# Two buffers for the exponents of weight halves, and their sums in the PSUM buffer of the weighted values, in an attention and feed-forward kernel

## The chip, the cores and the metric

The kernel runs on one core of one Trainium2 chip. The metric is the device time of one execution in microseconds (us). The change is judged by the median of several runs against the kernel before.

## What is computed

The reference draws `q`, `k`, `v` of 8 batches, 8 heads, 576 rows and 64 columns in fp32, and three weights `w_gate` and `w_val` (512 x 1536) and `w_out` (1536 x 512), and computes

```python
scores = (1 / 8) * q @ k.T                          # per batch and head
kth    = 32nd largest of each row of scores
attn   = softmax over the entries >= kth
x      = (attn @ v), heads side by side             # 4608 x 512
out    = (sigmoid(x @ w_gate) * (x @ w_val)) @ w_out
```

The weights reach the kernel as float64, two 32-bit words for each number.

## The kernel before, in words

The engines are TensorE (PE; its weight loads are the separate row PEld), VectorE (DVE), ScalarE (ACT), GpSimd (POOL) and SyncE (SP), which issues most loads. Each has an instruction queue of its own and works through it in order.

**Attention.** A step is one tile of 128 query rows of two heads. PE forms the scores (`pss`, L298 or L316), ACT evicts them (`s`, L302 or L324), DVE finds the leading values (L394 to L400), ACT and POOL count and mask what lies under them (L407, L413, L414), DVE takes the 32nd largest (`kths`, L421), ACT and DVE form the masked exponentials (`e`, L332, L337), and PE transposes them (`pt`, L432), which ACT evicts into a ring (L438). When the tiles of a block are there, `weigh` multiplies them by the values on PE into the PSUM tile `po` (L480, L481). DVE reads `po` and divides by the row sums (`xf`, L485), and ACT and POOL split the result into a high part `xh` (L504) and a rest `xl` (L505).

**Feed-forward network.** For 384 tokens at a time PE forms `pz` (L540 to L542), ACT and DVE evict it (L547, L550), ACT and POOL split the product (L551, L552), and PE multiplies by the output weights (`po_0_0_0` and the like, L564 to L566).

**Splitting the weights.** There are 18 weight tiles of two halves each, 36 halves in all, and each is split once, in the first 245 us or so. One half is 128 x 512 numbers of two words, loaded by SP into `wraw` (three buffers). `split_front` works on it as follows: ACT scales the upper word (`wbits`, L190), DVE shifts it into place and puts in the sign (L191, L192), DVE cuts the exponent out of it into the tile `wpower` (L193), ACT turns the lower word into a number (L195), POOL multiplies that number by the exponent in two pieces (L197), and ACT takes the high part (L198). `split_back` sums on PE in three matmul groups into one PSUM tile `wrest`: the bits times the identity (L205), the high part times -1 (L206), and the product of POOL times 2^-52 (L207). ACT evicts the sum (L209, issued with high priority), and the finished half is stored to DRAM (L210).

**PSUM.** The pool `ps_f` has three buffers and holds, in turn, `wrest`, `pz` and the output product of the network. The pool `ps_o` has one buffer and holds the weighted values `po` of `weigh` (L464). A new tile waits until the reader of the buffer's last tile has finished: L209 for `wrest`, L547 or L550 for `pz`, L485 for `po`.

**Order of the work.** The order on PE is written by hand (`tc.manual_schedule`): `split_back` is called between other pieces of work, and its three groups stand in PE's order where it is called. The order on ACT, DVE, POOL and SP is found by a scheduler, which takes into account when buffers come free and which calls are marked `urgent()`.

Of the kernel before, what the change touches and what calls it, by code (L numbers as in the profile page):

```python
# [10 lines left out]
F32 = mybir.dt.float32  # L11
# [3 lines left out]
F32R = mybir.dt.float32r  # L15
BF16 = mybir.dt.bfloat16
FP8 = mybir.dt.float8e4
AF = mybir.ActivationFunctionType
# [12 lines left out]
def tile_topk_attention_then_gated_ffn(  # L31
# [8 lines left out]
    nc = tc.nc  # L40
    P = 128
    B, H, _, S = k.shape
# [10 lines left out]
    M = NP * P  # L53
# [36 lines left out]
    bi = ctx.enter_context(tc.tile_pool(name="bi", bufs=4))  # L90
    b2 = ctx.enter_context(tc.tile_pool(name="b2", bufs=2))
    bk = ctx.enter_context(tc.tile_pool(name="bk", bufs=2 * NP))
    bv = ctx.enter_context(tc.tile_pool(name="bv", bufs=3))
    bs = ctx.enter_context(tc.tile_pool(name="bs", bufs=4))
    bq = ctx.enter_context(tc.tile_pool(name="bq", bufs=3))
    bqr = ctx.enter_context(tc.tile_pool(name="bqr", bufs=4))
    bkr = ctx.enter_context(tc.tile_pool(name="bkr", bufs=2))
# [6 lines left out]
    ps_o = ctx.enter_context(tc.tile_pool(name="ps_o", bufs=1, space=bass.MemoryType.PSUM))  # L104
    ps_f = ctx.enter_context(tc.tile_pool(name="ps_f", bufs=3, space=bass.MemoryType.PSUM))

    ident = const.tile([P, P], F32, tag="ident", name="ident")
# [26 lines left out]
    def behind_scores():  # L134
        return tc.issue_after(evicted[-1].ins) if len(evicted) < 12 else ExitStack()

    def urgent():
        return tc.high_priority() if stated else ExitStack()
# [10 lines left out]
    stored, splits, waiting, fetched, ticks, evicted, due, later, pinned, raw_loads = set(), {}, [], {}, [0], [], [], [], [], []  # L149

    pre = ExitStack()
    pre_pools = {n: pre.enter_context(tc.tile_pool(name=n, bufs=bufs)) for n, bufs in (("signs", 1), ("raw", 3), ("parts", 3), ("power", 1))}
    plus, minus = [pre_pools["signs"].tile([P, P], F32R, tag=t, name=t) for t in ("plus", "minus")]
    nc.scalar.activation(plus, ident, AF.Copy, scale=2.0**-52)
    nc.scalar.activation(minus, ident, AF.Copy, scale=-1.0)

    split_order = order[KEPT:LOADED] + order[:KEPT] + order[LOADED:]
# [10 lines left out]
    def load_raw(idx, i):  # L168
        raws[idx, i] = raw = pre_pools["raw"].tile([P, NP * P, 2], U32, tag="raw", name=f"wraw_{idx}_{i}")
        ins = load(raw.rearrange("p n t -> p (n t)"), w[idx][:, i * NP * P : (i + 1) * NP * P].bitcast(U32))  # L170
        raw_loads.append(ins.ins)

    def split_front(idx, i):

        if i == 0:
            splits[idx] = pools["w"].tile([P, 2, 2, NP, P], F32R, tag="w", name=f"wsplit_{idx}")
        at = halves_of_weights.index((idx, i))
        for ahead in halves_of_weights[at : at + 2]:
            if ahead not in raws:
                load_raw(*ahead)  # L180
        raw = raws[idx, i]
        low, top = raw[:, :, 0], raw[:, :, 1]
        pair = splits[idx][:, i].rearrange("p a c n -> p a (c n)")
        bits = pre_pools["parts"].tile([P, NP * P], F32, tag="bits", name=f"wbits_{idx}_{i}")
        frac = pair[:, 1]
        word = bits.bitcast(U32)
        power = pre_pools["power"].tile([P, NP * P], BF16, tag="power", name=f"wpower_{idx}_{i}")
        heads = bits.bitcast(U16).rearrange("p (n t) -> p n t", t=2)[:, :, 1]
        with behind_scores():
            nc.scalar.activation(bits, top.bitcast(F32), AF.Copy, scale=2.0**-112)  # L190
        nc.vector.tensor_scalar(word, word, 3, None, op0=ALU.logical_shift_left)  # L191
        nc.vector.scalar_tensor_tensor(word, top, 0x80000000, word, op0=ALU.bitwise_and, op1=ALU.bitwise_or)  # L192
        nc.vector.tensor_scalar(power.bitcast(U16), heads, 0xFF80, None, op0=ALU.bitwise_and)  # L193
        with behind_scores():
            nc.scalar.activation(frac, low, AF.Copy)  # L195
        for c in (slice(0, 2 * P), slice(2 * P, 4 * P)):
            nc.gpsimd.tensor_tensor(frac[:, c], frac[:, c].bitcast(F32), power[:, c], op=ALU.mult)  # L197
        nc.scalar.activation(pair[:, 0], bits, AF.Copy)  # L198
        waiting.append((idx, i, pair, bits, ticks[0]))

    def split_back():
        idx, i, pair, bits, _ = waiting.pop(0)
        frac = pair[:, 1]
        rest = ps_f.tile([P, M], F32, tag="f", name=f"wrest_{idx}_{i}")
        nc.tensor.matmul(rest, ident, bits, start=True, stop=False)  # L205
        nc.tensor.matmul(rest, minus, pair[:, 0], start=False, stop=False)  # L206
        nc.tensor.matmul(rest, plus, frac, start=False, stop=True)  # L207
        with urgent():
            nc.scalar.activation(pair[:, 1], rest, AF.Copy)  # L209
        nc.scalar.dma_start(w_split[idx][:, i], pair.bitcast(F32))  # L210
        if i == 1:
            stored.add(idx)
# [23 lines left out]
    def next_front():  # L236
        while len(waiting) > 2:
            split_back()
        split_front(*due.pop(0))
# [94 lines left out]
    def masked(J, s, kth, st, e, nm, place=None):  # L334

        for j in range(J):
            nc.vector.scalar_tensor_tensor(  # L337
                e[:, j], s[:, j], kth[j], e[:, j], op0=ALU.is_ge, op1=ALU.mult, accum_out=st[:, 4 + j : 5 + j]
            )
        nc.vector.tensor_scalar(st[:, 4 : 4 + J], st[:, 4 : 4 + J], 1e-9, None, op0=ALU.add)  # L340
        if place is not None:
            x, k, rows = place
            invs = inverses[x]
            sums = st[:, 4:6] if J == 2 else st[:, 4:5].to_broadcast([P, 2])
            nc.vector.reciprocal(invs[:, k:8:4], sums)
            if k == 3:
                turned_invs = b6[0].tile([P, 32], F32, tag="invt", name=f"invt_{nm}")
                nc.vector.transpose(turned_invs, invs)
                for x in range(4):
                    nc.sync.dma_start(rows[:, 32 * x : 32 * x + 32], turned_invs[32 * x : 32 * x + 8])  # L350
            return e, None
        nc.vector.reciprocal(st[:, 6 : 6 + J], st[:, 4 : 4 + J])
        inv = bi.tile([P, P], F32, tag="inv", name=f"inv_{nm}")
        nc.gpsimd.tensor_copy(
            inv.rearrange("p (j d) -> p j d", j=J), st[:, 6 : 6 + J].unsqueeze(2).to_broadcast([P, J, P // J])
        )
        return e, inv
# [19 lines left out]
    def select(J, s, col, nm, place):  # L377
# [42 lines left out]
        for j in range(J):  # L420
            nc.vector.max(kths[:, at[j] : at[j] + 8], u[:, j])  # L421
        yield masked(J, s, [kths[:, a + 7 : a + 8] for a in at], st, e, nm, place)

    def turn(e, inv, i, et, nm):
# [85 lines left out]
    def ffn(nm0, xs, t0, width, early, last):  # L510
# [7 lines left out]
        def load(idx):  # L518
            if not (t0 == 0 and early):
                return stored_weight(idx, nm0)  # L520
            first_weights(order.index(idx))
            while idx not in stored:
                if not waiting:
                    next_front()
                split_back()
            return fetched[idx]
# [72 lines left out]
    def run(general):  # L599
# [160 lines left out]
        for n in range(len(steps) + 3):  # L760
# [6 lines left out]
            if splitting:  # L767
                split_front(*fronts.pop(0))
# [24 lines left out]
            else:  # L793
# [9 lines left out]
                for t, chunk in enumerate(chunks):  # L803
                    ticks[0] += 1
                    if not fronts and not splitting:
                        if waiting and ticks[0] - waiting[0][4] > 3:
                            split_back()
                        if due and len(waiting) < 3:
                            next_front()
                    if chunk is not None:  # L810
                        next(chunk, None)
                        while unfinished and t == 0:
                            weighted(*unfinished.pop(0))
                    elif 3 <= n:
                        weighed(n - 3)
                        if n == OPEN:
                            weighed(n - 2)
                    if t == 2 and splitting and len(waiting) > 1:
                        split_back()
                    if n != OPEN or t > 0:  # L820
                        more(begun + (goal - begun) * (t + 1) / len(chunks))
# [84 lines left out]
```

## Time and profile before

| quantity | value |
|---|---|
| median of 3 runs | 1576.34 us |
| lowest and highest run | 1575.83 and 1578.79 us |
| the profiled execution's own time | 1575.44 us |
| its span in the profile | 1573.6 us |
| PE busy, share of the span | 1500.9 us, 95% |
| DVE busy | 1289.7 us, 82% |
| ACT busy | 1151.0 us, 73% |
| POOL busy | 1106.5 us, 70% |

The span runs from the first to the last instruction of the profile. The profiled execution is a run of its own beside the three that give the median: 1575.44 us, 0.90 us below that median. In the views an idle time in brackets names the instruction on another engine that ended it.

### The profile page before, as it was taken

The page shows a single profiled execution, that of the slowest core. Times are in us where ns is not written, and L with a number is a line of the kernel's source. Part 1 is how long each engine was busy: PE and PEld are TensorE (multiplying, and loading weights), DVE is VectorE, ACT ScalarE, POOL GpSimd, SP SyncE. Part 2 cuts the span into 40 slices and gives each one's busy share as a digit, 9 for nine tenths or more (in the row PEclk, how much of TensorE's full clock was granted, in tenths as well). Part 3 has the DMA queues.
Part 4 walks back from the last instruction along what each step waited for, and adds up shares of the span by engine and source line. Part 5 has one row for each costly group of instructions (what it writes and reads, how often), then busy time and mean ns, then how long its engine had stood idle before and what let it go on. Part 6 is the DMA issues. An engine that isn't in the chain of part 4 may idle for free.

```text
span 1573.6 us, 33616 instructions
## 1 busy us (share of the span) xinstructions
PE 1500.9 (95%) x10242; PEld 1310.9 (83%) x10242; DVE 1289.7 (82%) x5996; ACT 1151.0 (73%) x2520; POOL 1106.5 (70%) x1656
## 2 busy tenths in 40 slices
PE   5777999999999999999999999999999999999998
PEld 2355768988898899888898899888898899889897
DVE  7988878899999788999888788999888788998001
ACT  6868987888687678777777778777777778777321
POOL 4657897698776876887775876887775876775312
PEclk9889999999999999999999999999999999999999
DMA  6426878778665676676565675676555666564575
GB/s 204 151 93 221 274 274 303 270 250 299 228 214 190 228 260 204 212 254 211 198 210 190 228 257 206 213 251 213 199 209 190 228 224 224 198 217 168 208 271 186
DMA packets 96240, 347.34 MB, mean 221 GB/s; under 512 B 13105, under 2 KB 33585, under 8 KB 68273
## 3 DMA queue, kind: packets, MB, share of 16 engines
q1 hardware_dynamic: 90864, 326.22, 60.4%
q10 hardware_dynamic: 5184, 18.88, 3.0%
q8 instruction: 83, 1.36, 0.4%
q14 instruction: 109, 0.88, 0.2%
HBM read 316.60 MB, written 28.45 MB: 219 GB/s over the span
## 4 chain that ended last, share of the span: by engine, by line
PE 63%; DVE 11%; POOL 4%; ACT 4%; issue 2%; DMA 2%; ACTq 0%; SPq 0%; DVEq 0%; POOLq 0%
PE pz L540 10%; PE pz L542 9%; PE pz L541 9%; PE pss L316 7%; PE po L480 7%; PE pt L432 5%; PE po L564 5%; PE po L566 5%; PE po L565 5%; DVE e L337 3%; DVE cand L394 3%; POOL u L413 2%; DVE kths L421 2%; DVE cand L400 1%; ACT under L407 1%
## 5 line engine op out<-in xcount | busy, mean ns | idle before, releaser
L413 POOL TENSOR_TENSOR u<-s,under 128x288 f32<-128x288 f32 x576 | 423.9, 760 | 128.8 <-ACT under L407 124.1
L540 PE MATMUL pz<-xh,w 128*128 128x384 f32 (+1 forms) x1152 | 404.3, 351 | 0.0
L394 DVE MAX8 cand<-s 128x8 f32<-128x72 f32 x2304 | 352.9, 217 | 38.1 <-ACT s L324 26.5
L542 PE MATMUL pz<-xh,w 128*128 128x384 f32 (+1 forms) x1152 | 377.4, 328 | 0.0
L541 PE MATMUL pz<-xl,w 128*128 128x384 f32 (+1 forms) x1152 | 376.9, 327 | 0.0
L407 ACT ACTIVATE under<-s,leads 128x576 fp8e4<-128x576 f32 x288 | 222.6, 773 | 103.8 <-DVE leads L398 97.0
L337 DVE SCALAR_TENSOR_TENSOR e<-s,kths,e 128x576 f32<-128x576 f32 x288 | 282.9, 990 | 15.0 <-ACT e L332 14.4
L421 DVE MAX8 kths<-u 128x8 f32<-128x584 f32 x288 | 219.3, 761 | 66.1 <-POOL u L414 63.6
L552 POOL TENSOR_TENSOR gl<-gf,gh 128x384 fp32r<-128x384 f32 (+1 forms) x156 | 156.3, 1002 | 121.1 <-ACT gh L551 118.1
L540 PEld LDWEIGHTS pz<-xh,w 128*128 128x128 f32 x1152 | 217.1, 188 | 5.7 <-DVE tops L398 1.3
L332 ACT ACTIVATE e<-s,st 128x576 f32<-128x576 f32 x288 | 208.9, 771 | 15.7 <-PE pt L432 10.7
L541 PEld LDWEIGHTS pz<-xl,w 128*128 128x128 f32 x1152 | 217.7, 189 | 0.8
L542 PEld LDWEIGHTS pz<-xh,w 128*128 128x128 f32 x1152 | 216.5, 188 | 0.0
L438 ACT ACTIVATE ring<-pt 128x384 f32<-128x384 f32 x336 | 163.5, 496 | 56.9 <-PE pt L432 56.0
L432 PE MATMUL pt<-ident,e 128*128 128x128 f32 x1152 | 191.9, 276 | 7.8 <-ACT ring L438 7.8
L432 PEld LDWEIGHTS pt<-ident,e 128*128 128x128 f32 x1152 | 147.2, 141 | 39.4 <-ACT ring L438 11.2
L564 PE MATMUL po<-w,gh 128*128 128x512 f32 x408 | 173.1, 424 | 1.2 <-DVE gf L550 1.2
L324 ACT ACTIVATE s<-pss 128x576 f32<-128x576 f32 x256 | 164.2, 641 | 8.8 <-PE pss L316 8.3
L316 PE MATMUL pss<-k,qh 128*128 128x288 f32 (+2 forms) x588 | 162.2, 294 | 8.2 <-ACT s L324 7.9
L550 DVE SCALAR_TENSOR_TENSOR gf<-gf,pz 128x384 f32<-128x384 f32 (+1 forms) x156 | 79.7, 511 | 102.6 <-PE pz L542 90.4
L565 PE MATMUL po<-w,gl 128*128 128x512 f32 x408 | 160.9, 394 | 2.8 <-POOL gl L552 2.8
L566 PE MATMUL po<-w,gh 128*128 128x512 f32 x408 | 161.3, 395 | 0.0
(115 smaller groups left out, 3315.8 us busy)
## 6 DMA issues: line engine op xcount, KB each, us to landing
w<-ws SPq DMA_DIRECT2D x216, 1024.0 KB
v<-in_v_dram SPq DMA_DIRECT2D x68, 320.0 KB
wraw<-in_w_dram SPq DMA_DIRECT2D x36, 512.0 KB
ws<-wsplit ACTq DMA_DIRECT2D x36, 512.0 KB
qraw<-in_q_dram SPq DMA_DIRECT2D x140, 128.0 KB
kraw<-in_k_dram SPq DMA_DIRECT2D x56, 288.0 KB
out_dram<-acc SPq DMA_DIRECT2D x36, 256.0 KB
invb<-rows SPq DMA_DIRECT2D x66, 128.0 KB
```

Source lines behind the costliest of these rows:

```text
L316: nc.tensor.matmul(ps[:, half, o : o + n], x[:K, h * P : (h + 1) * P], ks[h][:K, k0 : k0 + n], start=t == 0, stop=t == len(todo) - 1,)
L337: nc.vector.scalar_tensor_tensor(e[:, j], s[:, j], kth[j], e[:, j], op0=ALU.is_ge, op1=ALU.mult, accum_out=st[:, 4 + j : 5 + j])
L394: nc.vector.max(cand[:, j, 8 * g : 8 * g + 8], s[:, j, g * SEG : (g + 1) * SEG])
L413: nc.gpsimd.tensor_tensor(u[:, j, c], s[:, j, c], under[:, j, c], op=ALU.mult)
L421: nc.vector.max(kths[:, at[j] : at[j] + 8], u[:, j])
L432: nc.tensor.transpose(pt[:, c], ef[:, k0 : k0 + P], ident)
L540: nc.tensor.matmul(ps[:, R], wt[:, u, 0, d], xh[:, R], start=d == 0, stop=False)
L541: nc.tensor.matmul(ps[:, R], wt[:, u, 0, d], xl[:, R], start=False, stop=False)
L542: nc.tensor.matmul(ps[:, R], wt[:, u, 1, d], xh[:, R], start=False, stop=d == NP - 1)
L564: nc.tensor.matmul(outs[r], gh, wh, start=f == 0, stop=False)
L565: nc.tensor.matmul(outs[r], gl, wh, start=False, stop=False)
L566: nc.tensor.matmul(outs[r], gh, wl, start=False, stop=f == FG - 1)
```

## The change

Four edits:

1. The pool `power` of the exponent tiles gets two buffers in place of one.
2. `wrest` is taken from `ps_o`, which keeps its one buffer and now serves both `wrest` and the `po` of `weigh`. `ps_f`, with its three buffers, is left to `pz` and the output product.
3. The matrix `plus` (2^-52 on its diagonal) and the one ACT instruction that makes it go. The factor is put into the scale of L195, with its sign, and L207 multiplies by `minus`.
4. The tile `inv`, which holds reciprocals of row sums, moves from a pool of four buffers to one of three.

```diff
+    binv = ctx.enter_context(tc.tile_pool(name="binv", bufs=3))
...
-    pre_pools = {n: pre.enter_context(tc.tile_pool(name=n, bufs=bufs)) for n, bufs in (("signs", 1), ("raw", 3), ("parts", 3), ("power", 1))}
-    plus, minus = [pre_pools["signs"].tile([P, P], F32R, tag=t, name=t) for t in ("plus", "minus")]
-    nc.scalar.activation(plus, ident, AF.Copy, scale=2.0**-52)
+    pre_pools = {n: pre.enter_context(tc.tile_pool(name=n, bufs=bufs)) for n, bufs in (("signs", 1), ("raw", 3), ("parts", 3), ("power", 2))}
+    minus = pre_pools["signs"].tile([P, P], F32R, tag="minus", name="minus")
...
-            nc.scalar.activation(frac, low, AF.Copy)
+            nc.scalar.activation(frac, low, AF.Copy, scale=-(2.0**-52))
...
-        rest = ps_f.tile([P, M], F32, tag="f", name=f"wrest_{idx}_{i}")
+        rest = ps_o.tile([P, M], F32, tag="o", name=f"wrest_{idx}_{i}")
...
-        nc.tensor.matmul(rest, plus, frac, start=False, stop=True)
+        nc.tensor.matmul(rest, minus, frac, start=False, stop=True)
...
-        inv = bi.tile([P, P], F32, tag="inv", name=f"inv_{nm}")
+        inv = binv.tile([P, P], F32, tag="inv", name=f"inv_{nm}")
```

The number of instructions stays the same but for the one of edit 3. PE's order stays the same too; what moves there is what an instruction waits for. The orders of ACT, DVE, POOL and SP differ from some 60 us to some 290 us of the profile and are the same behind that.

**PE, the second half of weight tile 4** (its `wrest` starts at 122.44 us in the profile). `w_first` and `wsplit` are weights, `xh`, `xl` inputs of the network, `e_3_0` exponentials to be transposed; in brackets stands whose signal the instruction waits for. Before:

```order
L541 MATMUL pz_0_3_0_1503<-xl_3_1200,w_first_1254 128x256
L542 MATMUL pz_0_3_0_1503<-xh_3_1199,w_first_1254 128x256
L205 MATMUL wrest_1_1540<-wbits_1_1392,ident 128x512 [waits DVE_49]
L206 MATMUL wrest_1_1540<-wsplit_1364,minus 128x512
L207 MATMUL wrest_1_1540<-wsplit_1364,plus 128x512 [waits Pool_49]
L432 MATMUL pt_3_0_1_1546<-ident,e_3_0_1147 128x128 [waits Activation_49]
L432 MATMUL pt_3_0_1_1546<-ident,e_3_0_1147 128x128 x2
L540 MATMUL pz_0_3_1_1551<-xh_0_686,w_first_1254 128x256 [waits Activation_49]
```

With the change:

```order
L541 MATMUL pz_0_3_0_1504<-xl_3_1201,w_first_1255 128x256
L542 MATMUL pz_0_3_0_1504<-xh_3_1200,w_first_1255 128x256
L205 MATMUL wrest_1_1541<-wbits_1_1393,ident 128x512 [waits Activation_49]
L206 MATMUL wrest_1_1541<-wsplit_1365,minus 128x512
L207 MATMUL wrest_1_1541<-wsplit_1365,minus 128x512 [waits Pool_49]
L432 MATMUL pt_3_0_1_1547<-ident,e_3_0_1148 128x128 [waits PE_49]
L432 MATMUL pt_3_0_1_1547<-ident,e_3_0_1148 128x128 x2
L540 MATMUL pz_0_3_1_1552<-xh_0_687,w_first_1255 128x256
```

L205 of the second half waited for DVE's eviction of a `pz` and now waits for ACT, the eviction of the first half's sum; the wait of L540 for ACT is gone.

**ACT, the keys of heads 1_2 and 1_3** (near 202 us in the profile). `qh`, `k` are copies of loaded queries and keys, `ring` the transposed exponentials. Before:

```order
L324 ACTIVATE s_4_2_2483<-pss_4_2_0_2484 128x576
L284 ACTIVATE qh_4_0_2639<-qraw_4_0_2637 128x256
L195 ACTIVATE wsplit_2494<-wraw_0_2398 128x512
L198 ACTIVATE wsplit_2494<-wbits_0_2497 128x512
L195 ACTIVATE wsplit_2494<-wraw_1_2495 128x512
L190 ACTIVATE wbits_1_2518<-wraw_1_2495 128x512
L209 ACTIVATE wsplit_2375<-wrest_0_2510 128x512
L438 ACTIVATE ring<-pt_2_3_0_2528 128x384
L265 ACTIVATE k_1_2_2813<-kraw_1_2_2811 128x576
```

With the change:

```order
L324 ACTIVATE s_4_2_2484<-pss_4_2_0_2485 128x576
L284 ACTIVATE qh_4_0_2640<-qraw_4_0_2638 128x256
L265 ACTIVATE k_1_2_2814<-kraw_1_2_2812 128x576
L195 ACTIVATE wsplit_2495<-wraw_0_2399 128x512
L198 ACTIVATE wsplit_2495<-wbits_0_2498 128x512
L195 ACTIVATE wsplit_2495<-wraw_1_2496 128x512
L265 ACTIVATE k_1_3_2820<-kraw_1_3_2818 128x576
L190 ACTIVATE wbits_1_2519<-wraw_1_2496 128x512
L209 ACTIVATE wsplit_2376<-wrest_0_2511 128x512
```

The two copies of keys, L265, stand ahead of the eviction L209 of `wrest_0`, where the first of them stood behind it.

**DVE, the division of the weighted values of block 11** (near 182 us in the profile; `kths_4_0` needs `u_4_0` of POOL). Before:

```order
L191 TENSOR_SCALAR wbits_1_2180<-wbits_1_2180 128x512
L192 SCALAR_TENSOR_TENSOR wbits_1_2180<-wraw_1_2147,wbits_1_2180 128x512
L485 TENSOR_TENSOR xf_11_0_2203<-po_11_2192,ring 128x128 x2
L191 TENSOR_SCALAR wbits_0_2298<-wbits_0_2298 128x512
L192 SCALAR_TENSOR_TENSOR wbits_0_2298<-wraw_0_2178,wbits_0_2298 128x512
L193 TENSOR_SCALAR wpower_1_2181<-wbits_1_2180 128x512
L550 SCALAR_TENSOR_TENSOR gf_1_3_2161<-gf_1_3_2161,pz_1_3_1_2212 128x256
L421 MAX kths<-u_4_0_2454 128x8
```

With the change:

```order
L191 TENSOR_SCALAR wbits_1_2181<-wbits_1_2181 128x512
L192 SCALAR_TENSOR_TENSOR wbits_1_2181<-wraw_1_2148,wbits_1_2181 128x512
L193 TENSOR_SCALAR wpower_1_2182<-wbits_1_2181 128x512
L191 TENSOR_SCALAR wbits_0_2299<-wbits_0_2299 128x512
L192 SCALAR_TENSOR_TENSOR wbits_0_2299<-wraw_0_2179,wbits_0_2299 128x512
L193 TENSOR_SCALAR wpower_0_2300<-wbits_0_2299 128x512
L421 MAX kths<-u_4_0_2455 128x8
L485 TENSOR_TENSOR xf_11_0_2204<-po_11_2193,ring 128x128 x2
```

Both cuts of exponents, L193, move up, and L485 moves behind the search L421.

## Rows read from the trace of the kernel before

**Rows 1.** Windows: stretch, its length, busy us of each engine, clock, DMA share, GB/s.

```profile
120.00:160.00 40.00, 32.05 (x165) 20.95 (x164) 35.47 (x123) 34.58 (x71) 31.21 (x44) 1.00 0.65 216
160.00:200.00 40.00, 38.34 (x215) 28.00 (x214) 35.05 (x112) 36.22 (x76) 33.15 (x45) 1.00 0.82 278
200.00:240.00 40.00, 37.22 (x201) 26.95 (x200) 30.39 (x86) 34.08 (x70) 36.06 (x48) 1.00 0.81 276
240.00:280.00 40.00, 38.92 (x341) 34.51 (x340) 31.87 (x167) 31.32 (x78) 29.43 (x56) 1.00 0.85 299
...
400.00:800.00 400.00, 394.72 (x2750) 355.32 (x2749) 357.09 (x1707) 307.81 (x684) 303.47 (x449) 1.00 0.63 220
```

**Rows 2.** Waits, 110 to 250 us: us in total, times, longest.

```profile
DVE wpower L193 <- POOL wsplit L197: 8.9, 10, 2.4
...
PE wrest L205 <- DVE gf L550: 6.4, 5, 2.4
...
PE pz L540 <- ACT wsplit L209: 3.7, 3, 2.1
...
PE wrest L207 <- POOL wsplit L197: 1.8, 3, 1.1
...
PE wrest L205 <- ACT wsplit L209: 1.4, 2, 1.0
```

**Rows 3.** Timeline of PE: start, us, instruction, idle before it and releaser.

```profile
120.08 1.02 PE L205 MATMUL wrest<-wbits,ident 128*128 128x512 f32 x2
...
121.16 0.39 PE L207 MATMUL wrest<-wsplit,plus 128*128 128x512 f32 x1
...
122.44 1.02 PE L205 MATMUL wrest<-wbits,ident 128*128 128x512 f32 x2
...
133.69 1.13 PE L205 MATMUL wrest<-wbits,ident 128*128 128x512 f32 x2 [2.42 <-DVE gf L550]
...
205.47 1.13 PE L205 MATMUL wrest<-wbits,ident 128*128 128x512 f32 x2
...
210.04 0.43 PE L480 MATMUL po<-ring,v 128*64 128x256 f32 x1
...
243.44 0.43 PE L480 MATMUL po<-ring,v 128*64 128x256 f32 x1
```

**Rows 4.** Timeline of ACT, the same columns.

```profile
125.66 0.61 ACT L209 ACTIVATE wsplit<-wrest 128x512 fp32r<-128x512 f32 x1
...
136.72 0.57 ACT L209 ACTIVATE wsplit<-wrest 128x512 fp32r<-128x512 f32 x1
...
202.25 0.41 ACT L284 ACTIVATE qh<-qraw 128x256 fp32r<-128x256 f32 x1
...
204.83 0.58 ACT L209 ACTIVATE wsplit<-wrest 128x512 fp32r<-128x512 f32 x1
...
207.25 0.69 ACT L265 ACTIVATE k<-kraw 128x576 fp32r<-128x576 f32 x1 [1.46 <-DMA kraw<-in_k_dram]
...
213.77 0.60 ACT L209 ACTIVATE wsplit<-wrest 128x512 fp32r<-128x512 f32 x1
```

**Rows 5.** Timeline of DVE near 182 us.

```profile
181.76 0.48 DVE L485 TENSOR_TENSOR xf<-po,ring 128x128 f32<-128x128 f32 x2
...
186.79 0.77 DVE L421 MAX8 kths<-u 128x8 f32<-128x584 f32 x1 [1.08 <-POOL u L414]
```

**Rows 6.** Timeline of PE, after a wait of 2.60 us.

```profile
105.85 0.58 PE L541 MATMUL pz<-xl,wsplit 128*128 128x256 f32 x1 [2.60 <-POOL xl L505]
...
106.44 0.41 PE L540 MATMUL pz<-xh,wsplit 128*128 128x256 f32 x1
...
106.65 0.41 PE L541 MATMUL pz<-xl,wsplit 128*128 128x256 f32 x1
...
109.77 0.28 PE L542 MATMUL pz<-xh,wsplit 128*128 128x256 f32 x1
...
109.89 0.28 PE L540 MATMUL pz<-xh,wsplit 128*128 128x256 f32 x1
```

## The prediction, made blind

> **What bounds the kernel now.** I read the busy times by stretch first. From 240 us on PE is busy for 38.92 us of 40, and for 394.72 of the 400 us behind 400 [rows 1]; the orders of all engines are the same there before and with the change. So whatever the change does, it does ahead of some 250 us, and a shift that PE has there is carried to the end nearly whole. Between 120 and 240 us the same view shows PE idle for 7.95, 1.66 and 2.78 us of each 40, with POOL at 33.15 and 36.06 and ACT at 36.22 and 34.08 of 40 in the last two [rows 1]. Here the weights are split, and here the change acts.
>
> Then I read the waits of 110 to 250 us [rows 2]. PE waits 6.4 + 3.7 + 1.4 = 11.5 us for readers of the three buffers of `ps_f` (a sum for the eviction of a `pz`, a `pz` or a sum for the eviction of a sum), and 1.8 us for POOL's product (L207). Together that is 13.3 us, all that PE loses in this stretch. DVE waits 8.9 us in ten pieces before it cuts an exponent (L193), since the one `wpower` is still read by POOL.
>
> Last I read the timeline around the sums. The sums come in pairs: L205 of one starts at 120.08, its L207 ends at 121.16 + 0.39 = 121.55, so that a sum takes 1.47 us, and the next starts at 122.44, 0.89 us behind that [rows 3]. Their evictions come far later: the first at 125.66 for 0.61 us [rows 4].
>
> **The change part by part.**
>
> *Second buffer for `wpower`, -8.9 us on DVE, nothing by itself on PE.* The waits on DVE go. What follows from L193 is POOL's product and then L207, for which PE waited 1.8 us in all [rows 2]. POOL is the engine that is full there (6.85 and 3.94 us idle in 160 to 240 us [rows 1]), and it has as many products as before. I leave POOL's times as they are.
>
> *`plus` goes, the scale goes into L195.* One ACT instruction less at the start, L195 and L207 with the same shapes: 0. The pool of `inv`: 0 on PE, whose order keeps all its rows; the work that hides a later `inv` is the step of attention between its making and its use.
>
> *The sums leave `ps_f`.* Gain: the 11.5 us of waits above go, and with the 1.8 us for POOL where PE comes later anyway, 13.35 us is the most that PE can win (the same waits added one by one from the timeline).
>
> *The sums come to the one buffer of `ps_o`.* Cost: each sum, and each `po`, must now wait for the reader of the one before. The nearest rows for its size are the starts of the sums and the ends of their evictions. The second sum, at 122.44, must wait for 125.66 + 0.61 = 126.27 and gets 3.8 us [rows 3, 4]. The sum at 133.69 had waited 2.42 us for a `pz`; now it waits for an eviction that came at 136.72 [rows 3, 4]. The `po` at 210.04 stands right behind a sum whose eviction came at 213.77 [rows 3, 4].
>
> I took PE through the stretch in this way, from the sum at 120.08 to the `po` at 243.44, 32 tiles in `ps_o` and some `pz` between. A tile arrives at its old start, less the wait that goes, plus the shift that PE has by then; it starts when the reader before it has ended; and L207 never starts before POOL's product did. Unknown is where an eviction comes when PE is late. ACT's queue is in order, and L209 stands in it behind evictions of PE's other output, which move with PE, and behind the splitting's own work, which doesn't. Bounds: if readers keep their old times, or start at once behind a sum that is late, 14.5 us of new waits come against 13.35 that go, +1.1 us. If the readers move by three quarters of PE's shift, +8.9. If they move with it in full, the waits feed each other up to +31; but for that ACT would need to be without slack, and it is idle for 3.78 and 5.92 us of two stretches of 40 [rows 1]. I take one half, since about as much of the work ahead of an L209 belongs to the splitting as to PE's output: 17.4 - 13.35 = +4.0 us.
>
> *The order that the scheduler finds.* Two places. On ACT the copies of keys L265 now stand right behind L284 (202.25 + 0.41 = 202.66) and ahead of the eviction that came at 204.83. The keys were there at 207.25, when ACT had already waited 1.46 us for them [rows 4]. If the load comes no earlier, ACT stands still for 207.25 - 202.66 = 4.6 us in place of 1.46, and L209 comes behind five more pieces of work of about 0.65 us, at about 210.3. The sum at 205.47 [rows 3] waits for it: 3.5 us there, part of which the `po` behind it would have waited anyway. In the same walk the shift at the end is then +4.8 in place of +4.0 (bounds +2.9 and +10). On DVE L485 of block 11 stands behind L421, whose operand came at 186.79, and had been done at 181.76 + 0.48 [rows 5]. It delays the ACT copy of that tile and the work queued behind it by up to 186.79 + 0.77 - 181.76 = 5.8 us; the next sum in `ps_o` came only 8 us behind that `po`, so I put PE's loss at 0 and keep this as a reason for not taking the lower bound.
>
> The Trainium skill, page "TensorE: Matmul & The Clock Gate", section "Architectural detail: the array is 16× 32×32, not 1× 128×128", says that only TensorE can pull weight loads ahead, while the queues of ScalarE, VectorE and GpSimd keep strict order. It speaks against the change, since a copy of keys that waits holds up each eviction behind it; by it the 4.6 us of ACT would be lost in full for all work queued there, and the sum would be the +4.8 and not the +4.0. The row of L265, with its idle time of 1.46 us, agrees as far as it goes [rows 4].
>
> *Ahead of 110 us* the sums stand farther apart and PE waits for other things; I take 0, and up to +1.5 for two `po` that follow a sum closely.
>
> Sum: between +4.0 and +4.8, taken as +4.6, on the profiled execution's own 1575.44: **1580.0 us**. That is 3.7 us, 0.23%, above the median of the runs shown, which lies 0.90 us above the profiled execution.
>
> **The rivals.**
>
> *A. The waits go and few come back: faster.* Once PE is late, its sums find the bits and products ready, and ACT, freed of the old pattern, evicts at once; DVE has 8.9 us more. For it: the waits of rows 2 are real and at the bound. Against it: the pairs 0.89 us apart [rows 3], and POOL. It decides if L209 comes within about 1 us of its sum's end; the first one came 4.1 us behind it (125.66 against 121.55). With no new wait PE could win 13.35; POOL's products can come earlier by at most POOL's idle time, 6.85 + 3.94 us in 160 to 240 [rows 1]. Half of that is -5: 1570.4.
>
> *B. An exchange of waits.* Readers keep their times, the load of keys comes earlier with SP's changed order: +1.1, or a little below 0 where DVE's time helps POOL: 1576.5.
>
> *C. The waits feed each other.* Readers move by three quarters of the shift, keys as above: +10, 1585.5. It decides at `po` behind a sum at 179 and 210 us, where shifts of 5 to 8 us would be seen.
>
> *D. The clock.* Behind a wait of 2.60 us at 105.85 matmuls of `pz` follow each other by 0.21 us, some 3 us later by 0.12 [rows 6]: half the clock, 1.2 in place of 2.4 GHz. Between 120 and 240 us the granted clock was 1.00 [rows 1] with a longest wait of 2.4 us [rows 2]. The new waits of 3.5 to 5 us could bring such a fall: some 2.5 us at half pace cost about 1.2 us each, three of them 3.7: 1583.7. The same page of the Trainium skill, section "A second HAM failure mode: psum-queue depth-cycling", tells of a kernel in which TensorE's short idle times between groups of matmuls that cycle through PSUM made the clock go up and down. The window at 1.00 with 11.5 us of such waits doesn't bear it out so far.
>
> That the edits do not take effect is no rival: PE's rows show the changed waits.
>
> **How the numbers follow.** About 0.2%, 3.2 us, is what a measurement can tell from no change. Forecast, with its own range of 1577.5 to 1584: 0.45. A 0.23, B 0.20, C 0.08, D 0.04. The forecast's lower quarter, with B and a little of A, lies within 0.2% of 1576.34. So: faster 0.22, same 0.30, slower 0.48. The range reaches from A's 1570.4 to beyond C and the first 1.5 us of the early stage, 1570 to 1587; C's full lock-step of +31 is left out.
>
> **What would show it.** Right: in the waits of 110 to 250 us PE's L205 waits for L209 with 10 to 18 us, waits of L540 for L209 are gone, `po` L480 waits for L209 near 182 and 214 us; DVE's wait of L193 for L197 is gone; ACT's L265 waits over 3 us near 203 us; PE's rows behind 250 us come about 4 us later and keep their distances. Wrong: L209 within 1 us of its sum, PE idle between 120 and 240 us below 10 us, or a shift that changes behind 250 us, where I count none.

## The result and the profile of the changed kernel

The change makes the kernel slower: 1591.87 us (median of 4 runs, 1589.15 to 1592.53) against 1576.35 us, a ratio of 1.0096 (95% interval 1.0083 to 1.0109), some 15.5 us. The direction was forecast; the size, 3.7 us, was not, and the range ended at 1587. The profiled execution took 1592.2 us, its span is 1590.4 us.

The busy times by stretch of the changed kernel, in the columns of [rows 1]:

```profile
120.00:160.00 40.00, 33.55 (x162) 21.94 (x159) 34.60 (x122) 33.55 (x69) 30.28 (x44) 0.91 0.61 213
160.00:200.00 40.00, 34.37 (x178) 24.53 (x178) 32.08 (x99) 30.35 (x61) 27.08 (x38) 0.87 0.69 227
200.00:240.00 40.00, 34.13 (x165) 23.67 (x164) 29.20 (x79) 30.55 (x61) 30.60 (x43) 0.96 0.82 270
240.00:280.00 40.00, 37.14 (x287) 30.66 (x286) 30.60 (x131) 31.01 (x73) 29.68 (x51) 1.00 0.80 263
...
400.00:800.00 400.00, 393.94 (x2805) 355.09 (x2803) 359.28 (x1714) 306.56 (x685) 306.74 (x454) 1.00 0.64 223
```

Behind 400 us nothing has changed. From 120 to 240 us PE is no less busy than before in the first stretch and 4.0 and 3.1 us less in the next two, and the granted clock, 1.00 there before, is 0.91, 0.87 and 0.96.

The stretch that counts runs from the first sum of the main part (120.08 us before, 121.54 now) to the `po` that ends it (243.44 and 259.39). Its windows, before and then now:

```profile
120.08:243.44 123.36, 109.88 (x584) 76.93 (x582) 104.17 (x338) 107.30 (x219) 103.70 (x143) 1.00 0.76 255
```

```profile
121.54:259.39 137.85, 117.05 (x583) 81.63 (x581) 109.17 (x335) 109.15 (x220) 102.54 (x148) 0.93 0.71 236
```

It takes 137.85 us in place of 123.36, 14.49 more. PE's busy time there grew from 109.88 to 117.05, by 7.17 us, though it runs the same matmuls; the rest, its idle time, grew from 13.48 to 20.80, by 7.32 us. A further 1.46 us lie ahead of the stretch. Behind it the distance of PE's rows to those before is 15.9 us up to 290 us and 16.7 us at the end. The last 0.8 us can't be put down to the change: in a second profile of the same kernel (further down) the distance falls there, from 15.0 to 13.8 us.

The waits of the changed kernel, 110 to 266 us (us in total, times, longest):

```profile
PE wrest L205 <- ACT wsplit L209: 16.9, 9, 3.9
...
ACT gf L547 <- PE pz L542: 6.2, 2, 5.6
...
DVE xf L485 <- PE po L481: 4.7, 4, 1.9
...
ACT wbits L190 <- PE wrest L205: 4.1, 5, 1.2
ACT k L265 <- DMA kraw<-in_k_dram: 4.1, 4, 1.5
...
PE po L480 <- ACT wsplit L209: 3.9, 3, 2.5
...
DVE wpower L193 <- POOL wsplit L197: 0.5, 1, 0.5
```

All that PE waits for in the stretch is now L209: 16.9 + 3.9 = 20.8 us, and of the waits of [rows 2] on PE none is left. DVE's 8.9 us for the exponent have become 0.5. ACT waits 6.2 us for PE's `pz`, and DVE 4.7 us for PE's `po`.

The dearest place is the sum at 177.77 us of the kernel before, with the `po` of block 11 behind it. PE there, in the columns of [rows 3]:

```profile
178.62 1.02 PE L205 MATMUL wrest<-wbits,ident 128*128 128x512 f32 x2
...
179.71 0.40 PE L207 MATMUL wrest<-wsplit,minus 128*128 128x512 f32 x1
...
185.10 2.07 PE L205 MATMUL wrest<-wbits,ident 128*128 128x512 f32 x2 [3.94 <-ACT wsplit L209]
...
187.40 0.63 PE L207 MATMUL wrest<-wsplit,minus 128*128 128x512 f32 x1
188.72 0.69 PE L480 MATMUL po<-ring,v 128*64 128x256 f32 x1 [0.69 <-ACT wsplit L209]
...
189.20 0.63 PE L480 MATMUL po<-ring,v 128*64 128x256 f32 x1
```

And ACT:

```profile
181.71 0.68 ACT L265 ACTIVATE k<-kraw 128x576 fp32r<-128x576 f32 x1 [1.19 <-DMA kraw<-in_k_dram]
182.30 0.64 ACT L195 ACTIVATE wsplit<-wraw 128x512 fp32r<-128x512 uint32 x1
...
184.46 0.58 ACT L209 ACTIVATE wsplit<-wrest 128x512 fp32r<-128x512 f32 x1
...
188.06 0.60 ACT L209 ACTIVATE wsplit<-wrest 128x512 fp32r<-128x512 f32 x1 [0.18 <-PE wrest L207]
...
194.23 0.38 ACT L547 ACTIVATE gf<-pz 128x256 f32<-128x256 f32 x1 [5.57 <-PE pz L542]
194.51 0.41 ACT L504 ACTIVATE xh<-xf 128x256 fp32r<-128x256 f32 x1
```

The first sum ends at 179.71 + 0.40 = 180.11. ACT stands 1.19 us for keys, then has four pieces of the splitting ahead of L209, which starts at 184.46: PE waits 3.94 us. The next sum then takes twice its time (L205 2.07 us in place of 1.02), the `po` waits for its eviction, and its matmuls, two at a time, follow each other by 0.48 us at first and then 0.42, against 0.21 before. Meanwhile ACT stands 5.57 us at L547, whose `pz` PE computes only behind that `po`. PE waits for ACT, and then ACT for PE. Here PE falls from 3.9 to 12.0 us behind the kernel before.

### The profile page after: what moved, and what is told of

The parts are those of the page before. It is cut to its first block, busy times and chain, and to the rows that moved or that the text cites. A ratio compares the mean times of both kernels' runs of the same rounds, so it can differ in the third digit from the quotient of the medians.

```text
span 1590.4 us, 33619 instructions
## 1 busy us (share of the span) xinstructions
PE 1510.5 (95%) x10242; PEld 1316.2 (83%) x10242; DVE 1295.0 (81%) x5996; ACT 1151.5 (72%) x2519; POOL 1099.2 (69%) x1656
## 4 chain that ended last, share of the span: by engine, by line
PE 66%; DVE 15%; POOL 7%; ACT 6%; issue 3%; DMA 2%; SPq 0%; POOLq 0%; ACTq 0%; DVEq 0%
PE pz L540 10%; PE pz L541 10%; PE pz L542 10%; PE po L480 7%; PE pss L316 7%; PE pt L432 5%; PE po L564 5%; PE po L565 5%; PE po L566 5%; POOL u L413 4%; DVE cand L394 3%; DVE e L337 3%; DVE kths L421 3%; DVE cand L400 1%; ACT under L407 1%
## 5 line engine op out<-in xcount | busy, mean ns | idle before, releaser
L540 PE MATMUL pz<-xh,w 128*128 128x384 f32 (+1 forms) x1152 | 404.4, 351 | 0.0
L421 DVE MAX8 kths<-u 128x8 f32<-128x584 f32 x288 | 219.1, 761 | 68.5 <-POOL u L414 66.1
L540 PEld LDWEIGHTS pz<-xh,w 128*128 128x128 f32 x1152 | 217.1, 188 | 5.5 <-DVE tops L398 1.1
L550 DVE SCALAR_TENSOR_TENSOR gf<-gf,pz 128x384 f32<-128x384 f32 (+1 forms) x156 | 79.7, 511 | 101.5 <-PE pz L542 88.7
```

Source lines behind the costliest of these rows:

```text
L540: nc.tensor.matmul(ps[:, R], wt[:, u, 0, d], xh[:, R], start=d == 0, stop=False)
```

## The experiments

Each is timed against the kernel before on the same chip. "Stretch" is the one named above. Lines of the code move by up to 11 in some kernels: the eviction of the sum is then L210, L211, L212 or L218, and L205 is L206, L207 or L214.

**All edits but the shared buffer.**

```diff
-        rest = ps_o.tile([P, M], F32, tag="o", name=f"wrest_{idx}_{i}")
+        rest = ps_f.tile([P, M], F32, tag="f", name=f"wrest_{idx}_{i}")
```

> The changed kernel, but the sums stay in the three buffers of ps_f (edits 1, 3 and 4 alone). Theory: the whole loss of 15.5 us comes from the one buffer of ps_o, so this kernel gives 1572 to 1578 us, and PE's waits of L205 and L540 for the readers of ps_f are back at 9 to 13 us. Rival: the loss comes from the other orders on ACT, DVE and SP or from the pool of inv with three buffers; then it stays above 1584 us.

Measured: 1573.74 us, ratio 0.9985 (0.9976 to 0.9995). Its waits, 110 to 250 us:

```profile
PE wrest L205 <- DVE gf L550: 4.0, 4, 1.6
...
PE wrest L207 <- POOL wsplit L197: 2.5, 3, 1.1
...
PE wrest L205 <- ACT wsplit L209: 2.2, 4, 1.0
...
DVE wpower L193 <- POOL wsplit L197: 0.9, 1, 0.9
```

The theory holds: the loss is edit 2's alone, and the rest of the change is a small gain. PE's waits for readers of `ps_f` are 4.0 + 2.2 = 6.2 us, less than the 9 to 13 expected.

**The shared buffer alone.**

```diff
-        rest = ps_f.tile([P, M], F32, tag="f", name=f"wrest_{idx}_{i}")
+        rest = ps_o.tile([P, M], F32, tag="o", name=f"wrest_{idx}_{i}")
```

(on the kernel before)

> The kernel before with edit 2 alone: the sums in ps_o, one exponent buffer, plus kept. Theory: 1588 to 1596 us, L205 waits for L209 with 14 to 20 us between 110 and 266 us, clock below 0.95 in two of the three stretches of 40 us from 120 to 240. Rival (the other edits carry the loss): within 4 us of the kernel before. If it is clearly slower than the change, the second exponent buffer paid for a part.

Measured: 1593.36 us, ratio 1.0118 (1.0095 to 1.0141). The clock is 0.91, 0.96 and 0.91, and PE's largest wait, 110 to 266 us:

```profile
PE wrest L205 <- ACT wsplit L209: 15.4, 9, 3.7
```

The whole loss is here. The interval overlaps that of the change, so this run doesn't show that the other edits paid for a part.

**Only first halves in the shared buffer.**

```diff
-        rest = ps_o.tile([P, M], F32, tag="o", name=f"wrest_{idx}_{i}")
+        rest = (ps_o if i == 0 else ps_f).tile([P, M], F32, tag="of"[i], name=f"wrest_{idx}_{i}")
```

> The changed kernel, but only the first half of each weight tile is summed in ps_o; the second halves stay in ps_f, so the two sums of a pair never share a buffer. Theory (a pair's second sum waits for the first one's eviction): L205's waits for L209 fall from 16.9 us to under 6, the clock stays at 0.98 or above from 120 to 240 us, and the time is 1574 to 1582 us. Rival (ACT and POOL are late as a whole, whichever buffer): above 1586 us.

Measured: 1574.68 us, ratio 0.9990 (0.9980 to 0.9999). PE's waits, 110 to 266 us:

```profile
PE po L480 <- ACT wsplit L209: 6.0, 2, 3.8
PE wrest L207 <- POOL wsplit L197: 2.0, 1, 2.0
```

L205 waits for no eviction at all any more, and the loss is gone, although 18 sums still pass the buffer of `po` and two `po` wait 6.0 us for them. So the loss hangs on the second sums of the pairs being in that buffer. This run also halves the number of sums in it; the runs that move the pairs, below, tell the two apart. The clock was lower than expected, 0.96 in each of the three stretches, and here that did not show in the time.

**Matmuls in the places of the waits.**

```diff
+    def fill(n, nm):
+        spare = ps_f.tile([P, M], F32, tag="f", name=f"spare_{nm}")
+        for _ in range(n):
+            nc.tensor.matmul(spare.rearrange("p (c n) -> p c n", c=NP), minus, minus.unsqueeze(1).to_broadcast([P, NP, P]), start=True, stop=True)
+
+    FILLS = {"4_1": 15, "13_1": 7, "8_1": 16, "9_1": 10, "0_13": 10}
...
+        if f"{idx}_{i}" in FILLS:
+            fill(FILLS[f"{idx}_{i}"], f"{idx}_{i}")
         rest = ps_o.tile([P, M], F32, tag="o", name=f"wrest_{idx}_{i}")
...
+        if nm in FILLS:
+            fill(FILLS[nm], nm)
         po = ps_o.tile([P, 4 * P], F32, tag="o", name=f"po_{nm}")
```

> The changed kernel with 58 matmuls of 128x512 that nobody reads, in a free buffer of ps_f, ahead of four sums and one po where PE waited for 1.95 to 3.94 us, about as long as these waits. Theory: half of the loss is the clock that falls behind these waits. PE then runs at a granted clock of 0.97 or above between 120 and 240 us and the time falls to 1583 to 1587 us. If the clock cost nothing beside the waits: 1590 us or above, since the matmuls take PE's time and give none.

Measured: 1590.81 us, ratio 1.0088 (1.0071 to 1.0105); the clock is 1.00 in all three stretches. The expected 1583 to 1587 us did not come; the time is the one expected if the clock costs nothing beside the waits. The stretch takes 134.45 us, 3.4 less than in the changed kernel, but this profile is 4.6 us later than that one when the stretch begins, so both were run again side by side.

> The changed kernel once more, unaltered, so that the next two are compared with it on the same chip: 1588 to 1594 us. From the first sum behind 110 us to the po that ends the stretch (137.85 us in its first profile) 136 to 140 us, of which PE sits idle 19 to 23 us.

Measured: 1590.97 us, ratio 1.0103 (1.0079 to 1.0127); the stretch takes 135.72 us, a little less than expected, with 20.9 us of idle time.

> The kernel with 58 unread matmuls in the places of the waits once more. If the first profile tells the clock's price rightly, the stretch from the first sum to the po that ends it takes 133 to 136 us at a granted clock of 1.00, 2 to 5 us less than in the changed kernel, and the time is 1 to 4 us below it. If the clock is free beside the waits, the stretch takes as long as in the changed kernel.

Measured: 1586.76 us, ratio 1.0080 (1.0058 to 1.0101). The stretch in the two profiles, the changed kernel and the filled one:

```profile
122.75:258.47 135.72, 114.84 (x584) 80.78 (x582) 108.46 (x335) 108.81 (x220) 102.73 (x148) 0.95 0.70 240
```

```profile
120.65:254.40 133.75, 122.12 (x642) 87.85 (x640) 108.37 (x335) 108.80 (x220) 102.87 (x148) 1.00 0.72 244
```

And PE's waits in the filled one, 120 to 255 us:

```profile
PE wrest L214 <- ACT wsplit L218: 8.2, 8, 1.6
PE po L491 <- ACT wsplit L218: 2.2, 2, 1.6
PE wrest L214 <- DVE xf L496: 0.9, 1, 0.9
```

The added matmuls take 14.1 us, of which 1.0 us overlaps other matmuls. So PE's own work is 122.12 - 13.0 = 109.1 us in place of 114.84: the clock had cost 5.8 us. (In the kernel before, at 1.00, it was 109.88.) The rest of the stretch, added matmuls and waits, is 133.75 - 109.1 = 24.7 us in place of 20.9. Of 5.8 us gained, 3.8 are waited away, and the stretch is 2.0 us shorter. The first profiles of the two kernels give 7.9 us gained, 4.5 waited away and 3.4 left (the rest is 25.3 us in place of 20.8). The added matmuls hide in the waits: only at two of the five places does PE go on later than the eviction lets it, by 0.8 and 0.1 us in the second profile. The intervals of the two ratios overlap in both comparisons, so the gain in time, 1.1 and 4.2 us by the medians, is not settled beyond "a few us". The clock is a real but small part; the readers set the pace.

**Pairs moved apart, and moved together.**

```diff
+        backs.append(ticks[0])
...
-                        if waiting and ticks[0] - waiting[0][4] > 3:
+                        if waiting and ticks[0] - waiting[0][4] > 3 and ticks[0] - backs[-1] > 2:
```

(`> 4` in the second kernel; there many sums are forced out just behind another)

> The changed kernel with PE's order written so that a sum is called only when three steps of the order or more lie behind the last one: the first pair of the main stretch is 24 rows of PE's order apart in place of 10, though some later pairs still are 4 to 8 apart. Theory (PE and ACT in lock-step over the one buffer, so what counts is PE's own work between two tiles in it): L205's waits for L209 fall from 16.9 to 8 to 13 us and the time to 1580 to 1588 us. Rival (what counts is that 40 tiles pass one buffer, wherever they stand): 1590 to 1593 us.

Measured: 1588.83 us, ratio 1.0084 (1.0066 to 1.0103). PE's waits, 110 to 280 us:

```profile
PE wrest L207 <- ACT wsplit L211: 6.6, 5, 2.3
PE po L568 <- ACT wsplit L211: 4.8, 3, 2.8
PE pz L544 <- ACT wsplit L211: 4.7, 3, 2.8
PE po L482 <- ACT wsplit L211: 3.2, 2, 2.5
PE wrest L207 <- DVE xf L487: 1.6, 2, 0.9
```

L205 (here L207) waits 6.6 us for L209, less than the 8 to 13 expected, and 1.6 us for L485. The time did not follow: it lies above the 1580 to 1588 us of the theory and below the range of the rival. 9.5 us of waits are new, where the network needs a weight (L568, L544) whose sum now comes too late. Moving sums apart trades one wait for the other.

> The changed kernel with the same rule at five steps, which makes sums pile up and come out in pairs of 3 rows of PE's order in place of 6 to 12. Theory (lock-step): each of some 11 pairs now pays nearly the whole time from a sum's end to the end of its eviction, 2 to 4 us; L205's waits for L209 rise to 25 to 40 us, the time to 1598 to 1615 us. Rival (place in the order is not what counts): 1590 to 1593 us.

Measured: 1606.86 us, ratio 1.0199 (1.0180 to 1.0217). PE's largest wait, 110 to 280 us:

```profile
PE wrest L207 <- ACT wsplit L211: 29.2, 12, 4.2
```

In 13 of the 14 pairs of the main part the second sum now stands on PE directly behind the first one, where 3 to 23 other matmuls, mostly 6 to 10, had stood between them. The same number of tiles passes the buffer and the loss doubles. The theory holds: the place in PE's order decides. The clock, 0.83 between 160 and 200 us, may have a part in it.

**First halves evicted by VectorE.**

```diff
         with urgent():
-            nc.scalar.activation(pair[:, 1], rest, AF.Copy)
+            if i == 0:
+                nc.vector.tensor_copy(pair[:, 1], rest)
+            else:
+                nc.scalar.activation(pair[:, 1], rest, AF.Copy)
```

> The changed kernel with the sums of first halves evicted by VectorE in place of ScalarE; the buffer stays as it is. Theory: the waits are long because L209 stands in ACT's order behind loads of keys and behind PE's own output; DVE's order has other things ahead, so the delay from a sum's end to its eviction changes, and with it the time, to 1578 to 1588 us if it gets below 1.5 us for the first halves. Rival (any reader in the queue of a busy engine is as late): PE's waits stay at 18 to 24 us and the time at 1588 us or above.

Measured: 1586.04 us, ratio 1.0067 (1.0048 to 1.0085). PE's waits, 110 to 280 us:

```profile
PE wrest L205 <- DVE wsplit L210: 9.5, 7, 2.2
PE po L483 <- ACT wsplit L212: 3.8, 2, 3.1
PE wrest L205 <- DVE xf L488: 1.9, 1, 1.9
PE wrest L205 <- ACT wsplit L212: 1.5, 1, 1.5
PE po L483 <- DVE wsplit L210: 1.0, 1, 1.0
```

From the end of a first half's sum to the start of its eviction it takes 0.97 us on the mean in place of 1.65 (14 sums, 110 to 260 us), the buffer's waits are 17.7 us in place of 20.8, and the time, from two runs, is some 5 us below the changed kernel's. The waits are just under the 18 to 24 us of the rival. A reader with less ahead of it helps, as expected, and does not cure it. Not all of the 5 us need come from the reader: the clock is 0.91, 1.00 and 1.00 here.

**One exponent buffer, sums in `ps_f`.**

```diff
-    pre_pools = {n: pre.enter_context(tc.tile_pool(name=n, bufs=bufs)) for n, bufs in (("signs", 1), ("raw", 3), ("parts", 3), ("power", 2))}
+    pre_pools = {n: pre.enter_context(tc.tile_pool(name=n, bufs=bufs)) for n, bufs in (("signs", 1), ("raw", 3), ("parts", 3), ("power", 1))}
```

(on the first experiment's kernel)

> The changed kernel with the sums in ps_f and one buffer of exponents: edits 3 and 4 alone. Theory (the gain of 2.1 us of edits 1, 3 and 4 together comes from DVE no longer waiting for POOL): 1575 to 1577 us, like the kernel before, with DVE's wait of L193 for L197 back at 8 to 9 us. Rival (the gain comes from the matrix that goes or from the pool of inv): 1573 to 1574.5 us.

Measured: 1575.59 us, ratio 0.9998 (0.9989 to 1.0007). The wait that came back, 110 to 250 us:

```profile
DVE wpower L193 <- POOL wsplit L197: 8.3, 9, 2.4
```

Without the second buffer the gain of the first experiment is gone. By the medians the second exponent buffer is worth about 2 us, but the intervals of the two ratios touch, so the size is not settled. The matrix that goes and the pool of `inv` are worth nothing that can be measured.

**One sum of 36 taken out of the shared buffer.**

```diff
+        out_of_po = (idx, i) == (8, 1)
-        rest = ps_o.tile([P, M], F32, tag="o", name=f"wrest_{idx}_{i}")
+        rest = (ps_f if out_of_po else ps_o).tile([P, M], F32, tag="f" if out_of_po else "o", name=f"wrest_{idx}_{i}")
```

> The changed kernel with one sum of 36, the second half of weight tile 8, in ps_f. In the changed kernel its wait of 3.94 us, the wait of 0.69 us of the po behind it and the slow matmuls there moved PE from 3.9 to 12.0 us behind the kernel before. If these 8 us are a price of that place, the time falls by 5 to 8 us, to 1584 to 1587 us. If PE, once early, only waits longer at the places behind it, less than 3 us come of it.

Measured: 1589.76 us, ratio 1.0090 (1.0073 to 1.0107), against 1.0103 (1.0079 to 1.0127) for the changed kernel run beside it. PE's waits, 121 to 258 us:

```profile
PE wrest L206 <- ACT wsplit L210: 16.6, 9, 3.7
PE po L481 <- ACT wsplit L210: 4.3, 2, 2.5
```

The dearest place is gone, and PE waits 16.6 + 4.3 = 20.9 us as before. What is won at one place is waited at the next ones: the second answer, less than 3 us, is the one that came.

## Why the prediction was wrong, step by step

*Where it acts* was right: all but 1.5 us arise between 120 and 260 us, and the shift is carried to the end.

*The second buffer for `wpower`, put at 0,* was too low by about 2 us: the wait went as forecast (8.9 to 0.5 us), and with the sums in `ps_f` the kernel gets something for it. It does not come by PE's waits for POOL: L207's waits for POOL are 2.5 us in the first experiment, where they had been 1.8. It comes by the readers of `ps_f`, for which PE waits 6.2 us in place of 11.5. That DVE, freed of its own wait, evicts `pz` earlier fits this (L550: 4.0 us in place of 6.4), but no run tests it alone.

*`plus`, the scale and `inv` at 0* were right (ratio 0.9998).

*The waits that go, 13.35 us,* were right: none of the 13.48 us of idle time is left.

*Two terms of the sum failed.* The sum made +4.6 us on the profile; PE is 15.9 us later behind the stretch. Of that, 7.3 us are waits (20.8 that came against 13.5 that went), 7.2 us are the clock, which the sum put at nothing, and 1.5 us lie ahead of the stretch.

*The waits that come: the step "I take one half" failed,* that the readers move by half of PE's shift because the splitting's own work ahead of an L209 doesn't move with PE. It gave 18.2 us with the keys. Measured were 20.8, at a clock that had slowed PE down and so shortened its waits; with the clock held up, matmuls and waits in their places were 24.7 and 25.3. In the prediction three quarters stands for 8.9 + 13.35 = 22.25 us, so the waits lie beyond the share of rival C. The profile shows the share itself. Over the 28 sums behind 110 us PE was 9.2 us late on the mean and the evictions 8.3 us, nine tenths of it: from the end of a sum to the start of its eviction it took 2.18 us before and takes 1.24 now. And the splitting's own work did move: L190, L195 and L198 came 7.7 us later on the mean where PE was 9.1 us late (73 rows between 125 and 242 us of the kernel before). ACT does not run on while PE waits. In the stretch its idle time that PE's work ended grew from 2.5 to 17.3 us: the 5.57 us at L547, and also 4.1 us of L190, a part of the splitting, whose buffer is only free when PE has read the bits of an earlier half. Before, 110 to 250 us, this wait of L190 was

```profile
ACT wbits L190 <- PE wrest L205: 1.4, 3, 0.7
```

I had seen ACT idle for 3.78 and 5.92 us of 40 and taken that for room to run ahead.

*The copies of keys* were the right place and too dear: ACT stood 1.49 us there, not 4.6, as the load came with ACT's own delay; the eviction behind it came 2.91 us behind its sum, where it had been 0.26, and PE waited 2.50 us for it, not 3.5:

```profile
215.59 0.69 ACT L265 ACTIVATE k<-kraw 128x576 fp32r<-128x576 f32 x1 [1.49 <-DMA kraw<-in_k_dram]
...
218.94 0.57 ACT L209 ACTIVATE wsplit<-wrest 128x512 fp32r<-128x512 f32 x1
```

ACT stood 5.57 us at L547 and started it at 194.23, with work of the splitting queued behind it. The bits that the next L198 reads were written by 188.78 + 1.07 = 189.85, and it ran at 197.32:

```profile
188.78 1.07 DVE L192 SCALAR_TENSOR_TENSOR wbits<-wraw,wbits 128x512 uint32<-128x512 uint32 x1
...
197.32 0.62 ACT L198 ACTIVATE wsplit<-wbits 128x512 fp32r<-128x512 f32 x1
```

The Trainium skill, page "TensorE: Matmul & The Clock Gate", section "Architectural detail: the array is 16× 32×32, not 1× 128×128", has ScalarE's queue in strict order, and the trace agrees; I had used that for the keys alone, and it held for everything ahead of an L209.

*L485 of block 11 at 0* was right, for another reason: DVE came to it before `po` was there.

```profile
190.78 0.77 DVE L421 MAX8 kths<-u 128x8 f32<-128x584 f32 x1
193.30 0.49 DVE L485 TENSOR_TENSOR xf<-po,ring 128x128 f32<-128x128 f32 x2 [1.75 <-PE po L481]
```

*The clock, rival D at 0.04 and at nothing in the sum,* came: 7.2 us of PE's busy time. I had argued that waits of 2.4 us left it at 1.00; the longest that came were 3.94 and 3.69. But it also fell behind waits of 1.95 and 2.50 us (0.57 from 146 to 150 and from 228 to 232 us), so the length of the last wait alone does not tell when it falls. As a price it was near the 3.7 us given, since most of the 7 us would otherwise be waited: holding it up shortened the stretch by 2.0 and 3.4 us in the two pairs of profiles. The Trainium skill, on the same page, section "A second HAM failure mode: psum-queue depth-cycling", tells of a clock that goes up and down with TensorE's short idle times between groups of matmuls that cycle through PSUM. The changed kernel's trace agrees as far as the clock is 0.91, 0.87 and 0.96 with 20.8 us of such waits; the kernel before, at 1.00 with 11.5 us of them, does not.

*Ahead of 110 us* the upper end came, 1.46 us: two `po` wait 0.98 and 0.21 us, and one sum 1.19 us for L485.

Rivals A and B are excluded. C had the right direction for the readers and was still too small, at +10. The first experiment's kernel, all edits but the shared buffer, is below both the kernel before and the changed one: 0.9985.

Left open: what part of the time, between some 1 and 4 us, the clock takes by itself, and why it fell where it did.

## What to carry to other kernels

When two users of PSUM are put into one buffer, look at the distance on PE between a tile and the next in that buffer, and compare it with the time from a tile's end to its eviction; tiles that come in pairs pay the difference each time. Do not take the reader's idle time as room: ask what stands ahead of the eviction in the reader's order, and if that is output of the waiting engine itself, or work that waits for it, count the new waits at nearly full length, and don't expect that removing one of them is worth its length.

## What was not expected of the hardware

Behind a wait of 3.94 us TensorE ran at half its clock for some 9 us, and matmuls of 128x256 followed each other by 0.42 us in place of 0.21. It also fell behind waits of 1.95 and 2.50 us, while in the same stretch of the kernel before waits of up to 2.42 us left the granted clock at 1.00. Unread matmuls in the place of the waits kept the clock at 1.00 with remaining waits of up to 2.1 us. Yet a clock that gave back 5.8 us of matmul time moved the end of the stretch by 2.0 us only.
